# Attention and gated MLP on one core: output products of chunks 1 and 2 by seven block products, scores and P V in one TensorE visit

## The chip, the core and the metric

The kernel runs on one core of a Trainium2 chip. A core has five engines with their own instruction streams: PE (TensorE, matrix products into PSUM), DVE (VectorE), ACT (ScalarE), POOL (GpSimd, which works on SBUF alone) and SP, which issues most of the DMAs. They wait for each other through semaphores. The metric is the device time of one execution in microseconds; lower is better.

## What is computed

A sparse attention over 8 batches, 8 heads, 576 positions and head dimension 64, whose output, put together as 4608 tokens of width 512, goes through an RMS norm and a gated MLP with 1536 hidden units:

```python
scores = scale * np.matmul(q, k.transpose(0, 1, 3, 2))
mask_local = (rel >= 0) & (rel < stride)                          # heads 0 to 3, stride 32
mask_strided = (rel >= 0) & (pos[None, :] % stride == pos[:, None] % stride)   # heads 4 to 7
attn = softmax(np.where(masks, scores, -1e9))
x = np.matmul(attn, v)                     # then [4608, 512]
xn = x / rms * rms_g
g = xn @ w_gate                            # [512, 1536]
silu = g * (1.0 / (1.0 + np.exp(-g)))
out = silu * (xn @ w_val) @ w_out          # [1536, 512]
```

## The kernel before

**Chunks and units.** The 4608 tokens are 9 chunks of 512 columns (c = 0 to 8). The hidden width is 12 blocks of 128 (u). Every operand of a large product is split into a high half and a low half (fp32r), and a product is three matmuls: high by high, low by high, high by low. A plain gate or value product of one u is 4 blocks of 128 x 3 = 12 matmuls of 512 columns; a plain output product of one u is 4 x 3 = 12.

**Chunks 0, 1, 2** (`for c in range(NS1)`, near the end of `attn_moe`) are done plainly. For each u: `slot_g` and `slot_v` form g and v in one PSUM bank each (`g`, `v`), ACT takes tanh and DVE forms h = 0.5 (1 + tanh(g/2)) g v in the tile `e`; `slot_h` splits h into `hh` (ACT) and `hl` (POOL, line 1045), and `slot_o` (line 1055) adds 4 x 3 matmuls of that u into four accumulator banks a0 to a3, which are held for the whole chunk.

**Pairs of chunks** (3, 4), (5, 6) and (7, 8) are done as 2 x 2 block products by a Strassen-like scheme with seven products in place of eight. `plain_pair(c, beside)` does the first two pairs, `pair_of_chunks(7)` the last. A pair has a gate and value stage of twelve quads, `quad(q)` (line 1822), each of seven products of 6 matmuls with operands A11, A12, S1, S2, S3, S4, A22 (S1 is the sum of the second chunk's parts, S2 = S1 - A11), and then an output stage (line 2053) of seven products, A11, A12, S1, S2, S4, S3, A22 in that order, each of 2 x 6 x 3 = 36 matmuls. The output stage needs every h of the pair, sums of them (`hsum`, line 2028), splits of them (`split`, lines 1968 to 1972), and weights transformed once into DRAM: `transform_gv` and `transform_o` do that on DVE, POOL and ACT, spread over chunks 1 and 2. A quad uses the banks (g, a0, a2) or (v, a1, a3) by turns.

**Attention** runs beside all this, in units (b, p, j), 96 of them. From unit 20 on (`BT`) two units go together: a visit of TensorE for their scores (line 564, `step_e`), the masked row maximum on DVE (570), exponentials on ACT (577), normalising (607, 609), a 32 x 32 transpose on DVE (620), moves by DMA (623), and later a visit for P V of four units (line 798, `step_o`). Both kinds of visit use the two banks b0 and b1 of the tile `pair`. The profile shows two passes for each of these matmuls. `rms(c, ...)` then squares, adds, takes the square root (943), four reciprocals (946) and four scalings (950) for the 512 tokens of a chunk.

**Order.** Lines 418 to 441 give every attention unit a slot for its scores (`starts`) and for its P V (`outs`); `before(s)` and `behind(s)` list them beside slot s. This listing settles the dependencies. The real order of the instructions on each engine, and which engine does an operation that has a choice, is read from the packed table `ORDER` by `Plan.order` (line 283), which takes any listed operation next that the table names. In an output stage `between()` lists two slots after each product.

Of the kernel before, what the change touches and what calls it, by code (L numbers as in the profile page):

```python
# [47 lines left out]
TOW = ((1, 2), (1, 6), (1, 10), (2, 0), (2, 4), (2, 8))  # L48
# [8 lines left out]
GOFF = 0  # L57
FP = 99
# [119 lines left out]
    "c-rk*X>1(ld49fQ?%CPddzZ`QeIMc_k`gaT6iJDcMCzbKilV67mK0gC9XqmO$98JNZX7sH8n<!cI=1ZCIqJra8@nwW2TkibXi=nT(55NcB0vH(Kz<bMpB89;"  # L178
    "wBIqa(x0LY;2;UA1*M(iop0Xbd7k&3*~vE645LJlDkU??{+ffOUc*SG(hD7_(3ta0(@&ghI_cY;aD(x&qvaRf>otMpJ6CzY7aibf%8dj!ug*GVirc@=O=KB&"
    "nStP40!puea)Q9XT@-HmQ3^sH2J!j1w0q5*A|EnbfY=tjZ`BGJamhs>?NaPbo+eg-;JDR5XUwB0d4#&~7dcH6jEDuf9~wLMps<azZbo*x_^&M~vc;S5kNtb|"  # L180
    "u(yf<1KSSSoA^Kl?p~9j-3o#qaGR#-4_(>~ez!$Tw*b7?_&xq^mVZ0j^k;b2$fi?ltPqCZ%dt0-8TJ=%zSj6w`i=J*-bil>UaP~a@6fKVf5rbow&S%|e42j#"
    "D=&I2U-XcC{&TpFmlD^XxBbsN_uGO0x!;8U{Fl6mr(W}({dE3%>oZR#U&)O=3p4S;W9Dzw`_Ce2eCjg~KT|fIHlF;AkH9PZ8o&0~NAsWjT=MVvC!RZz#r;p0"
    "*~hM>pY}g7!0vsjf{(fPl|M)yO*}>)xa;ym52HY@k~0_XyO#Xu6Q{}3IA^6E-9UIbq_rPFaE9Y*@#Lik{qo%xH*jC_GR_~nH+vT6@5I`vb06?maGIu<FP}@E"
    "-nfd~`bLn&;VX$#chB*Y2RF`N+J5}X#({%4y=@6A8#_)-Wowr=N^5&DxjM0b|L()6KX_o@F?MX_!J|jnkv+%Q=={NhN9K<oe)T}pAzb{|tt*S!1LwA^J~y-H"
    "z+PmQ=J%}aC0Jj<mV@($jKdh2U9$IM=f1xEd)PwP-d(%z?V3A@$+?M6y0&u%R(A}Lvq$Q;wQe4tIDQ;snAtHuf24UDyLjU^Oixd2UO@fWuC0spTV^m$7U#zn"
    "D|5q`8J#&hI*lE72ZI}RI59GD@tD;&)=vh{p4s%>@^|{t^Z5<z@6G+B>zPeI&UGfcJDkn~nWx&?m)f><W-#B@-pMd}S5vvM1$UA=9CD$<uhf#Dxuyng3%p8x"
    "ZS81-vr#te2GkX6Q814qN0G2H$BwM-O%Y@doP?7|?AtdJy3;3pc)pFmSsim${9xI4uHb;_zzF`_G7{f5;hLNq<_^o*jv8i|oFPjmhG`mOWcS#iaBjpTm}X0K"
    "5L3HQH|JcckgXxV{dLPG?JVy#f6+KGf??ikrv{v`BRs^<Bpoa=cqe)1`a$ZfV2;?cGa!`D&CSi@+`_E0OHi#my$<6TifaqSag5E`d28p+oXIlVuv>6*d?%Ks"
    "17LL2r@Q{ZdJF5s#x%FK!#Ly|nq>X~-w@;;fjw+fi(;hDAYd3Xw_Y0Vhr79V$Uyhm9=q!_SjW0cC|V{N(8z(MkuGyD+e6x&e)RP*f*zwA!irC}v$i&Dp)DAu"
    "z#w7$sGzr(pym$#0hEfY6)kz%)MPY*r0YOJp%Z*_J)cbvR|e7N)lQIc1V!Pf2eSos*jNIsutcs@AZCW9x#LjAeREU6qv+xwU1r!ugxjJ-b)JD*Rs$ghCb<ND"  # L190
    "QLI64!#SI5hdV{U*FCJcM~|AIM+jR!!IwoySVE1DWri9Dc~ZdPw5ZjAUFpf(40dLx!w@2aVxcb284&{6ZnyNe*{NO&CQFNCxiu}#s1%W`E7?KT`=EW7@7hV%"
    "wQbwAUD%d&Dug*05QIn5t5^w-u)|p-ofIX<T+gBlM+nT?oXahqLe4adFlE?`!>REG2*5jgb5=XQ-9+U~a|(@NO*5;d`&v<~NuXS;E22<FzJzo-4STd=r)|5o"
    "QYzWS(y(0^dZ%Cy4wP&^x6td`U$cMUxqmZbryRRCF%?YOey>*_jH0!YXsI2r(C<!~y;gn2Hb=_l%5Zkr>N)~*e;<}|Mo)KZl6SN;r&(i;dg-YtVt5neKN4`@"
    "=55%Sf3}t!nAo#_aZj+cU>fu0E)T{Gx4}qYPf`nW+z}iQ`Np3lgn;9{B$}N>6B^2}e!sRXE{4go!ki)#A|X<g@DUoX_#O>}D7V59*>oG>RN$l5gu_Mly$nTI"
    "=MflQfDhX2F6txjGFJLO-Bij7-J}&bmgRK@zHKEOtJzLimws&F!jIfaCGn57*ZgwXM9GHm^D^U%G2`}s2?CcTIQ!90t)DRahyO$jla2|u{+5sMr5}**e~%7P"
    "?tFJ>H^G3_3(}20=HJ2y`{p3pjPIkB68u#Y@RzjyJEE{a1OL+!YAWWpkT1Mr6hX2enN&WVLKX;K7T`*}`0|U_uV07%7I~8x_&u=K)9B><ciP&%6@H1b=4QOz"
    "(DViJhZbHySixIwSa|a_hS&MmUWG_1%rC#vX}<ggy!1!!cnxoV1K)JtcDcB98^za6^7>bdufpc!%U=Y0nY<W?MGDCTf$RC63(pyYjT({u>jm(C_`HR`Bk5-;"
# [24 lines left out]
    "MM~977f#CnlO8KW7E!LMv<g<S&T4i<F9~Q|W^w~ugz5}vGp$EN+akJD8p;ClDqb}bv>qwNRBq^NW7$EBES15VBvR2hib1EBM6EB1Hp;nRn(A242c;}162xGZ"
    "MT$xg$%BTV!UoaWqcvAus5FHWtxCFFTBcM9<&NrgH0B1;9HTmV1sW1#S8b7~x~lEoP)k)Go!H1ubuq4NScFWf3B%%6sM;yht|(@6PNMDT7L;nqS5)L0psLX`"
    "wK|P~$fIr?32@Ya;^^b<q;8-yt(Jy{i)54vm+IF*abKZ2aK@rAx#}BAWT@;&QMXl{M593El`Fy44K0FLd>v&p>bq38B%Ry1nR2bnygFBCYH_UvERrRSsCd3o"
    "nbHzh{nJXJ?x|N&c+{G5(+m?gIE9_KAx2{X<$83w`4qV^#^_cQflt#f%DtXDxMrD7K92`0xv4vpb~$c2H@U7Cjuo4sssSXnmw$}tc`S0iO7A#APDxapD%ce&"
    "6|^EgC~2f|%hG-_ooW@n?f}YT)o0aUOr!X8KIJe>dDJ%bI2tvkC@9L~K}a_^C~Ms{5z~xoazrR5T2V<nO=+t0xMx!uYXymxjFPJiiSGM1A0yH58ut{{=BgBk"
    "=uI@+Sk-UM$r$kZTWfH2_Lkvm<xpAEtx%6rEGoAabRL%;Rkgk`ZYi8;NX16+w62@O&GOG9p^jh|PxMOgBe{$QfoM3<-*F(CJ#kyolNRExeM3pr{H*7yDtRJo"
    ">ReKOW8RBqKULCL=#`Fw>vj<hKe_>^QAUwftfj^>)%YTD)KQWck~$gsc}G({R(x$z{nMc0)kIgn;}J&#0(#Vn;!t)n3DL+}<uK>*(-w~xW15ycQkEM)R#&Lu"
    "LOT#Wtq~skr4d1irlfwN;?e1<P}As<g-4L74ra=+m{HMFWE7DC#Z9#4k+kS98a>ddhgwACWx9Lo(UhwpSN7X@Sd9RwClwx<=rE#3BQ3$P+sX_)9xQGMn4Waw"
    "r^*QTnqpe?Slo}ujo&bM{A!n1H+l3NPc;kae*-sUL~j"  # L230
)


class Plan:

    LAT = LATC
# [13 lines left out]
    def op(self, eng, cost, at, fn, reads=(), writes=(), bytes_=0, rel=0.0, lock=(), tab=None, port=False, chain=False, also=None, early=0.0):  # L253
        i = len(self.ops)
        self.early.append(early)
        self.lift.append(0.0 if chain else self.boost)
        deps = set()
        for r in reads:
            if r in self.writer:
                deps.add(self.writer[r])  # L260
# [2134 lines left out]
```

## Time and profile before

| | us |
|---|---|
| runs | 3062.59, 969.14, 969.25 |
| median | 969.25 |
| the profiled execution | 968.01 |
| its span, first to last instruction | 966.1 |
| PE busy | 949.1 |
| DVE busy | 760.4 |
| ACT busy | 612.3 |
| POOL busy | 291.5 |

By the places of its lines in the trace, the attention of batch 0 fills the first 43 us, chunk 0 lasts to about 147, chunks 1 and 2 to about 397, the quads of pair 3 to 545 and its outputs to 602, pair 5 to 735 and 790, the last pair to the end. A duration that the profile gives to a matmul covers its whole passage; the distance between starts is what it costs in a row of them.

### The profile page before, as it was taken

How to read it: one execution, taken by the hardware profiler on the slowest of the kernel's cores; microseconds unless marked ns; L12 is line 12 of the kernel's file. 1: busy time of each engine (PE TensorE's matmuls, PEld its weight loads, DVE VectorE, ACT ScalarE, POOL GpSimd, SP SyncE). 2: the span in 40 equal slices, each digit the busy share in tenths (PEclk: the TensorE clock that was granted, in tenths of full speed). 3: DMA queues.
4: the chain of work that ended last, by engine and by line, in shares of the span. 5: the costliest groups of instructions: out<-in, count | busy, mean ns of one | idle time of the engine just before them, and what ended most of it. 6: DMA issues, size and time to landing. Idle time of an engine off the chain costs nothing.

```text
span 966.1 us, 16212 instructions
## 1 busy us (share of the span) xinstructions
PE 949.1 (98%) x5138; PEld 763.6 (79%) x5138; DVE 760.4 (79%) x1786; ACT 612.3 (63%) x1706; POOL 291.5 (30%) x286
## 2 busy tenths in 40 slices
PE   8999999999999999999999999999999999999998
PEld 6777777878876888788888788888877778888886
DVE  4889899878778889668856999955589997457882
ACT  6899999875569655675737883644378734333330
POOL 7333332353344541422213322200023330012340
PEclk9899999999999999999999999999999999999999
DMA  9999677665458448245664779675546794692551
GB/s 297 362 354 378 226 259 241 223 206 182 152 178 254 145 144 271 67 142 179 230 216 139 242 249 351 230 246 193 167 155 197 256 358 171 247 327 88 174 172 68
DMA packets 99381, 210.99 MB, mean 218 GB/s; under 512 B 11040, under 2 KB 40416, under 8 KB 99296
## 3 DMA queue, kind: packets, MB, share of 16 engines
q1 hardware_dynamic: 98528, 209.10, 63.6%
q10 hardware_dynamic: 768, 0.85, 0.3%
q8 instruction: 41, 0.67, 0.3%
q14 instruction: 44, 0.36, 0.1%
HBM read 158.99 MB, written 47.19 MB: 213 GB/s over the span
## 4 chain that ended last, share of the span: by engine, by line
PE 84%; DMA 5%; ACT 5%; DVE 3%; issue 1%; SPq 0%; POOL 0%; ACTq 0%; DVEq 0%; POOLq 0%
PE acc L1822 10%; PE g L1003 9%; PE acc L1055 9%; PE v L1003 9%; PE g L1822 7%; PE v L1822 6%; PE acc L2053 4%; PE pair L564 3%; PE pair L1433 3%; PE v L1433 3%; PE g L1433 3%; PE pair L798 3%; PE v L2053 2%; PE g L2053 2%; PE acc L1433 2%; PE v L1598 2%
## 5 line engine op out<-in xcount | busy, mean ns | idle before, releaser
L1003 PE MATMUL g<-xh,wg 128*128 128x512 f32 x288 | 92.7, 403 | 4.6 <-ACT srt L943 2.5
L1055 PE MATMUL acc<-or,hh 128*128 128x512 f32 x288 | 91.1, 398 | 0.0
L1003 PE MATMUL v<-xh,wv 128*128 128x512 f32 x280 | 88.2, 396 | 0.0
L1045 POOL TENSOR_TENSOR hl<-e,hh 128x512 fp32r<-128x512 f32 x36 | 49.0, 1362 | 116.9 <-ACT hh L1036 99.0
L1003 PEld LDWEIGHTS g<-xh,wg 128*128 128x128 f32 x288 | 52.1, 189 | 18.7 <-DVE e L1018 3.2
L577 ACT ACTIVATE pp<-pp,my 96x128 f32<-96x128 f32 (+2 forms) x146 | 56.8, 395 | 11.4 <-DVE my L570 11.3
L1055 PEld LDWEIGHTS acc<-or,hh 128*128 128x128 f32 x288 | 53.0, 188 | 12.8 <-issue 0.6
L1003 PEld LDWEIGHTS v<-xh,wv 128*128 128x128 f32 x280 | 51.5, 188 | 12.4 <-DVE e L1029 0.5
L1003 PE MATMUL g<-xl,wg 128*128 128x512 f32 x144 | 56.2, 390 | 0.0
L1055 PE MATMUL acc<-or,hl 128*128 128x512 f32 x144 | 56.1, 390 | 0.0
L577 ACT ACTIVATE pT<-pT,my 96x128 f32<-96x128 f32 (+2 forms) x130 | 50.4, 391 | 6.8 <-DVE my L570 6.6
L1003 PE MATMUL v<-xl,wv 128*128 128x512 f32 x140 | 54.6, 390 | 0.0
L883 POOL TENSOR_TENSOR ssq<-ssq,srt 128x512 f32<-128x512 f32 x21 | 29.5, 1404 | 50.6 <-ACT srt L878 47.8
L564 PEld LDWEIGHTS pair<-xx,xx 64*96 64x96 f32 (+2 forms) x552 | 31.9, 167 | 14.3 <-issue 9.2
L564 PE MATMUL pair<-xx,xx 64*96 64x128 f32 (+2 forms) x552 | 39.8, 281 | 0.7 <-ACT raw L843 0.7
L1036 ACT CAST hh<-e 128x512 fp32r<-128x512 f32 x36 | 22.4, 621 | 26.0 <-DVE e L1029 18.0
L607 ACT ACTIVATE pp<-pp,my 96x128 f32<-96x128 f32 (+2 forms) x114 | 36.3, 394 | 3.4 <-DVE my L596 3.1
L570 DVE CUSTOM_DVE_ANT_0 pp<-pair,cb 96x128 f32<-96x128 f32 (+2 forms) x146 | 32.8, 282 | 5.9 <-PE pair L564 5.9
L570 DVE CUSTOM_DVE_ANT_0 pT<-pair,cb 96x128 f32<-96x128 f32 (+2 forms) x130 | 29.2, 281 | 8.4 <-PE pair L564 8.3
L1018 DVE SCALAR_TENSOR_TENSOR e<-e,g 128x512 f32<-128x512 f32 x36 | 24.5, 680 | 11.2 <-ACT e L1016 10.8
L1003 PEld LDWEIGHTS g<-xl,wg 128*128 128x128 f32 x144 | 27.1, 188 | 6.1
L1055 PEld LDWEIGHTS acc<-or,hl 128*128 128x128 f32 x144 | 27.0, 188 | 5.8
(819 smaller groups left out, 2864.7 us busy)
## 6 DMA issues: line engine op xcount, KB each, us to landing
wv<-wsv SPq DMA_DIRECT2D x29, 512.0 KB, 5.6
or<-wos SPq DMA_DIRECT2D x48, 256.0 KB, 3.6
or<-tg SPq DMA_DIRECT2D x22, 512.0 KB, 6.1
th<-tg SPq DMA_DIRECT2D x21, 512.0 KB, 6.0
tl<-tg SPq DMA_DIRECT2D x21, 512.0 KB, 5.8
wg<-wsg SPq DMA_DIRECT2D x19, 512.0 KB, 8.0
xx<-in_qT_dram SPq DMA_DIRECT2D x31, 288.0 KB, 4.7
xx<-in_kT_dram SPq DMA_DIRECT2D x28, 288.0 KB, 4.2
```

The costliest lines, as they stand in the source:

```text
L564: nc.tensor.matmul(out=sp[h][:, t].rearrange("q x k -> q (x k)"), lhsT=qt[r, q0:q0 + m], rhs=kt[r, k0:k0 + P], start=True, stop=True)
L570: nc.vector.tensor_tensor_reduce(out=PX[x][:m, :, g0 + 2 * h + t], in0=sp[h][:, t], in1=mk[t], scale=-0.125, scalar=3.0e38, op0=ALU.add, o ...
L577: nc.scalar.activation(out=v, in_=v, func=AF.Exp, scale=-1.0, bias=mx2[z][:m, u, h, t:t + 1], accum_out=su2_[z][:m, u, h, t, 0:1])
L607: nc.scalar.activation(out=w, in_=w, func=AF.Copy, scale=mx2[z][:m_, y, h, t:t + 1])
L798: nc.tensor.matmul(out=po[64 * h:64 * h + 64, x * 32 * nx:(x + 1) * 32 * nx].rearrange("d (x q) -> d x q", q=32), lhsT=vt_of(vt, p)[:n, h, ...
L883: op("Pool", pool(CH), at, lambda e: (nc.vector if e == "DVE" else nc.gpsimd).tensor_tensor(out=ssq, in0=ssq, in1=roots["srt"], op=ALU.add ...
L1003: nc.tensor.matmul(out=out, lhsT=wt[:, w, sl], rhs=xhl[x, kc], start=(kc == 0 and i == 0), stop=(kc == KC - 1 and i == 2))
L1045: (nc.vector if n == "DVE" or h else nc.gpsimd).tensor_tensor(out=hl[h], in0=e, in1=hh[h].bitcast(F32), op=ALU.subtract)
L1055: nc.tensor.matmul(out=acc[t], lhsT=x[h][:, sl], rhs=wt[:, w], start=(u == 0 and i == 0), stop=(u == NU - 1 and i == 2))
L1433: nc.tensor.matmul(out=banks[bk], lhsT=w, rhs=X[a, k].tile(y), start=start and k == 0 and i == 0, stop=stop and k == 1 and i == 2, skip_gr ...
L1822: nc.tensor.matmul(out=banks[bk], lhsT=w, rhs=xtile(a, k, y), start=start and k == 0 and i == 0, stop=stop and k == 1 and i == 2, skip_gro ...
L2053: nc.tensor.matmul(out=banks[bks[j]], lhsT=w.tile(v, k, j), rhs=x.tile(k, y), start=start and n == 0 and i == 0, stop=stop and n == KT - 1 ...
```

## The change

Chunks 1 and 2 keep their plain gate and value products, but all of their h is kept in SBUF (`slot_h1`) and their output products become the seven-product output stage of the pairs, which is moved out of `plain_pair` into a function `outputs` of its own. Chunk 2 takes its units in the order 11, 10, 9, 0 to 8. The slots behind it move by twelve. g and v of chunks 1 and 2 alternate between banks a2, a3 and g, v. P V of units from 24 on goes to a0 and a1 (one tile, `acc01`), a2 and a3 become two separate tiles, and the quads of pairs 3 and 5 use a2 and a3 alone beside g and v. A score visit and a P V visit that fall into one slot are one PE operation. The output weights are no longer read again for chunks 1 and 2; `transform_o` reads them from DRAM. The root of a chunk goes through bank a1 in place of g. The table `ORDER` is new throughout.

```diff
-TOW = ((1, 2), (1, 6), (1, 10), (2, 0), (2, 4), (2, 8))
+TOW = (14, 17, 20, 23, 26, 29)
+TGW = (13, 15, 16, 18, 19, 21, 22, 24)
+VSP = (12.0, 16.0, 26.0, 12.0, 12.0, 30.0, 12.0, 20.0)
+PVD = 2
+FU = 24
...
-        acc23 = ps.tile([P, 2, 512], F32, name="acc23")
...
+    acc = [acc01[:, 0], acc01[:, 1]] + [ps.tile([P, 512], F32, name=f"acc{t}") for t in (2, 3)]
...
+    slots = [9.0] * 12 + [5.9] * 24 + [4.9] * 12 + [9.9] * 12 + [4.9] * 12 + [9.9] * 12 + [4.9] * 12
+    t_of = [sum(slots[:x]) for x in range(len(slots) + 1)]
+    visits = {}
+    for k, (i0, i1, sa, sb_) in enumerate(((BS, 36, 12, 24), (36, 60, 24, 48), (60, 84, 48, 72), (84, last + 1, 72, 96))):
+        n = (i1 - i0) // 2
+        ta, tb_ = t_of[sa] + VSP[2 * k], t_of[sb_] - VSP[2 * k + 1]
+        for x in range(n):
+            t = ta + (tb_ - ta) * x / n
+            visits[max(y for y in range(len(slots)) if t_of[y] <= t)] = [i0 + 2 * x, i0 + 2 * x + 1]
...
-            d = where[i + PG - 1 - (i - PP0) % PG if i < last - 7 else i + (last - i) % 2] + PVL
+            late = next(x for n, x in ((36, 22), (60, 45), (84, 69), (last + 1, 90)) if i < n)
+            d = min([x for x in visits if x >= max(s + PVD, NU + 1)] + [max(late, s + PVD)])
             outs[d] = outs.get(d, []) + [i]
...
-                m8 = pair[:m, :, 508:508 + nt]
+                for hs, pr in joint(pn):
+                    m8 = pr[:m, :, 508:508 + nt]
...
+        if beside_:
+            op("PE", SC0 + length + sum(x[2] for x in beside_), 0, lambda: [x() for x in [y[0] for y in beside_] + [values]],
+               reads=reads + [y for x in beside_ for y in x[1]], writes=wk + [("S", 0), ("T", 0)], lock=("b0", "b1") + locks[:len(units)])
...
-    def bank_of(c, key):
+    def bank_of(c, key, x=0):
...
-        return bank[key[0]], key[0]
+        n = (key[0], {"g": "a2", "v": "a3"}[key[0]])[x]
+        return banks[n], n
...
+    def slot_h1(c, u, x):
+        out, bk = bank_of(c, ("v", u), x)
...
+        op("DVE", dve(CH), 0, lambda: nc.vector.scalar_tensor_tensor(
+            out=htile1(u, c - 1), in0=e(), scalar=0.5, in1=out, op0=ALU.mult, op1=ALU.mult), reads=[bk, ek],
+            writes=[hkey1(u, c - 1)] + [k for k in first if k != hkey1(u, c - 1)])
...
-            p, q_, r = (("g", "a0", "a2"), ("v", "a1", "a3"))[z]
+            p, q_, r = (("g", "a3", "a3"), ("v", "a2", "a2"))[z] if q < 2 else (("g", "a2", "a3"), ("v", "a3", "a2"))[z]
...
-        for m in "125637":
+        for m in "126537":
...
+    for c in (1, 2):
+        for x, u in enumerate(range(NU) if c == 1 else order2):
+            s = NU * c + x
+            slot_g(c, u, x % 2)
+            slot_v(c, u, x % 2)
...
+            beside(s)
+            slot_h1(c, u, x % 2)
+            roots_of(s, "a1", "A01")
+            if s in tslots:
+                transform_gv(tslots[s])
+            if s in TOW:
+                transform_o(TOW.index(s))
...
+    outputs(1, lazy1, htile1, hkey1, beside, (0, 1, 2, 3, 4, 5),
+            {"a": ("wg1", "wv1", "wg3", "wv3", "wg4", "wv4"), "b": ("wg0", "wv0", "wg2", "wv2", "wg5", "wv5"),
+             "c": ("X0", "wv7", "wg8", "wv8", "th0", "tl0")}, ("wg6", "wv6", "wg7", "X1", "X2", "X3", "or4"),
+            ["wg5", "wv5", "wg6", "wv6", "wg7"] + list(H2), ["wv7", "wg8", "wv8"])
```

`outputs` holds the seven products as `plain_pair` had them, and its lists name where operands (a, b, c) and weights lie and which gate and value weights are given back (`early` before the last product, `late` after it). X1 to X3 are the tiles of the x operands of the plain products.

## Rows read from the trace of the kernel before

**Rows 1.** Stretches: length, busy PE, PEld, DVE, ACT, POOL (instructions), clock, DMA share, GB/s

```profile
147.00:272.00 125.00, 123.42 (x712) 99.00 (x713) 103.21 (x283) 92.77 (x294) 49.78 (x47) 1.00 0.61 201
272.00:397.00 125.00, 121.77 (x726) 96.81 (x725) 106.21 (x296) 85.15 (x264) 53.64 (x51) 1.00 0.58 189
...
545.00:602.00 57.00, 56.82 (x285) 46.05 (x284) 55.18 (x109) 35.23 (x86) 13.48 (x12) 1.00 0.84 285
...
39.00:50.00 11.00, 11.00 (x55) 8.91 (x51) 8.71 (x29) 8.27 (x28) 3.65 (x3) 0.53 0.96 331
```

**Rows 2.** Chain of waits: start us, us, what; one block of six matmuls

```profile
421.55 1.36 PE v L1822 x6
```

**Rows 3.** Waits of PE: who, for whom, us in total, times, longest

```profile
PE g L1003 <- ACT srt L943: 2.5, 2, 1.9
PE g L1003 <- DVE e L1018: 2.1, 2, 1.5
...
PE acc L1433 <- DMA wg<-wsg: 0.4, 1, 0.4
```

**Rows 4.** Stretches of one line alone, L1055 first, then L2053: busy PE (matmuls)

```profile
0.00:966.10 966.10, 114.48 (x432) 79.95 (x432) 0.99 0.64 218
...
0.00:966.10 966.10, 118.50 (x504) 93.92 (x504) 0.99 0.64 218
```

**Rows 5.** Groups: line, engine, operation, tiles, shapes, count, busy us, mean ns, idle

```profile
L1972 DVE TENSOR_TENSOR or<-wv,or 128x512 fp32r<-128x512 f32 x8 | 5.3, 678 | 0.3 <-ACT or L1968 0.3
...
L1107 DVE TENSOR_TENSOR tt<-wg 128x512 f32<-128x512 f32 x6 | 7.7, 1281 | 0.0
...
L1045 POOL TENSOR_TENSOR hl<-e,hh 128x512 fp32r<-128x512 f32 x25 | 34.0, 1362 | 66.7 <-ACT hh L1036 66.7
```

**Rows 6.** Timeline of PE, a score visit: start us, us, line, tiles, count

```profile
450.03 0.39 PE L1822 MATMUL v<-xl,th 128*128 128x512 f32 x1
450.35 1.12 PE L564 MATMUL pair<-xx,xx 64*96 64x128 f32 x16
451.40 0.98 PE L1822 MATMUL acc<-wg,wg 128*128 128x512 f32 x3
452.21 0.63 PE L1822 MATMUL acc<-wv,wg 128*128 128x512 f32 x2
```

**Rows 7.** Timeline of PE, a P V visit

```profile
769.51 0.84 PE L2053 MATMUL g<-tl,wv 128*128 128x512 f32 x3
770.28 0.88 PE L798 MATMUL pair<-pp,vt 128*64 128x96 f32 x16
771.09 0.96 PE L2053 MATMUL v<-tl,wv 128*128 128x512 f32 x3
771.89 0.40 PE L2053 MATMUL acc<-wv,wg 128*128 128x512 f32 x1
```

**Rows 8.** Timeline of PE in the prologue, scores followed by P V

```profile
17.01 0.38 PE L672 MATMUL pair<-wg,xx 128*126 128x126 f32 x2
17.23 0.38 PE L672 MATMUL pair<-wv,xx 128*126 128x126 f32 x2
17.55 0.55 PE L804 MATMUL acc<-xl,vt 128*64 128x96 f32 x8
```

**Rows 9.** Instructions of line 689: count, ns min/median/max, first and last start, forms

```profile
L689 DVE TENSOR_SCALAR mx<-acc x9: 157/158/161, 10.2 to 35.5; 96x4 f32<-96x4 f32 x5, 108x4 f32<-108x4 f32 x2, 108x2 f32<-108x2 f32 x2
```

**Rows 10.** Timelines of PE, ACT and DVE: last P V of chunk 6, root, operand S1

```profile
561.24 1.53 PE L798 MATMUL pair<-pT,vt 108*64 108x128 f32 x24
...
578.08 0.69 ACT L943 ACTIVATE srt<-acc,few 128x512 f32<-128x512 f32 x1
...
604.67 0.69 DVE L1729 TENSOR_TENSOR wv<-or,wv 128x512 fp32r<-128x512 f32 x1
```

**Rows 11.** Groups of DVE from 147 to 397 us: reciprocals and scalings of the roots

```profile
L946 DVE RECIPROCAL srt<-srt 128x128 f32<-128x128 f32 x16 | 14.2, 917 | 0.0
...
L950 DVE SCALAR_TENSOR_TENSOR raw<-raw,few,srt 128x512 f32<-128x512 f32 x16 | 11.5, 736 | 0.1
```

More of the change, by code (lines that the diff above doesn't have):

```diff
@@ L182 @@
[L182 to L185, printed above, removed]
@@ L251, in __init__, with op @@
         self.boost = 0.0
-    def op(self, eng, cost, at, fn, reads=(), writes=(), bytes_=0, rel=0.0, lock=(), tab=None, port=False, chain=False, also=None, early=0.0):
+    def op(self, eng, cost, at, fn, reads=(), writes=(), bytes_=0, rel=0.0, lock=(), tab=None, port=False, chain=False, also=None, early=0.0, extra=()):
         i = len(self.ops)
@@ L772, in step_t, with step_o @@
         op(*(("DVE", dve(2 * nt * m)) if i in EVD else ("ACT", act(2 * nt * m, True))), at + 1500,
[L773 to L775 removed]
+           lambda e: [nc.scalar.copy(out=dv[:, hs], in_=pr[:n, :, 256:256 + nt * m]) if e == "ACT" else
+                      nc.vector.tensor_copy(out=dv[:, hs], in_=pr[:n, :, 256:256 + nt * m]) for hs, pr in joint(pn)], reads=[TK], writes=[tk], lock=locks, also=[])
+    def step_o(units, beside_=()):
         flight.difference_update(units)
@@ L870, in square @@
             lead = p == (0 if c < NB - 1 else 2)
-            assert not (lead and busy)
+            assert not (lead and busy), (c, p, busy)
             busy.add(c)
@@ L1165, in attn_moe, with lent @@
     loan = {}
-    def lent(n):
-        if n not in loan:
-            loan[n] = sb.tile([P, CH], F32, name=n)
-        return loan[n]
+    def lent(n, x=0):
+        if (n, x) not in loan:
+            loan[n, x] = sb.tile([P, CH], F32, name=n)
+        return loan[n, x]
     def temps_of(z):
@@ L2046, in plain_pair @@
-        ended = set()
-        def oproduct(x, w, bks, start, stop):
-            for j in range(2):
-                for n, k in enumerate(KO):
-                    def fn(j=j, k=k, n=n):
-                        for i, (v, y) in enumerate(((0, 0), (1, 0), (0, 1))):
-                            nc.tensor.matmul(out=banks[bks[j]], lhsT=w.tile(v, k, j), rhs=x.tile(k, y), start=start and n == 0 and i == 0,
-                                             stop=stop and n == KT - 1 and i == 2, skip_group_check=True)
-                    op("PE", 680, 0, fn, reads=w.key(k) + x.keys(k), writes=bank_keys(bks[j]), chain=True)
@@ L2256, in scores_of @@
                 x[3]()
+            for i in units:
+                step_d(i)
             return
@@ new lines, in attn_moe @@
+    for u in range(NU):
+        at, s = T(0, u), u
+        before(s)
+        slot_g(0, u)
+        if u == NU - 1:
+            slot_v(0, u)
+            convert(1, at + CVO)
+        behind(s)
+        if u < NU - 1:
+            slot_v(0, u)
+        if u > 0:
+            slot_o(0, u - 1, at + SOO)
+        slot_h(0, u)
+        roots_of(s)
+    for c in (1, 2):
[3 more added lines that the diff above has]
+            slot_v(c, u, x % 2)
+            if c == 1 and x == 0:
+                slot_o(0, NU - 1, 0)
+            if c == 1 and x == NU - 1:
+                convert(2, 0)
+            beside(s)
+            slot_h1(c, u, x % 2)
+            roots_of(s, "a1", "A01")
```

670 lines of the change are left out of this document (341 added, 329 removed).

## The prediction

> **What bounds the kernel now.** The profiled execution took 968.0 us, its span is 966.1 us; the median of the three runs is 969.25 us, 1.2 us more, so a sum made against the profile should come out about a microsecond low against a run. I read the page's busy times first: PE is busy 949.1 us of the span (98%), DVE 79%, ACT 63%, POOL 30%. Busy PE is not useful PE, so the next view is the table by stretch [rows 1]: in the two stretches that hold chunks 1 and 2, PE is busy 123.4 and 121.8 of 125 us at a granted clock of 1.00. Then the chain of waits: a block of six 512-column matmuls advances it by 1.36 us [rows 2], 0.2267 us each, one behind the other; that is the unit of price below. Last the waits of PE [rows 3]: none totals more than 2.5 us. So from about 50 us on the kernel is a queue of matmuls: taking matmuls out shortens it, and making other engines busier costs nothing until PE waits for them. DVE is where that would begin, with 103.2 and 106.2 of 125 us in these stretches and 55.2 of 57 us in the output stage of pair 3, which is the pattern of the new stage; yet PE was busy 56.8 of those 57 us [rows 1].
>
> **Part 1, output products of chunks 1 and 2.** Now each chunk takes 144 output matmuls: L1055 has 432 for chunks 0, 1 and 2. A pair done by seven block products takes 252: L2053 has 504 for two pairs [rows 4]. 2 x 144 - 252 = 36 matmuls fewer, 36 x 0.2267 = **8.2 us** off PE. No other matmul of the MoE changes its count.
>
> The new work is elementwise: 7 products x 6 operands are split into high and low halves (42 casts, 42 subtractions, where 24 of each go), 24 sums of h, 8 copies and 6 merges out of PSUM for 8 evictions. At 0.68 us [rows 5] the 42 + 24 + 6 are 49 us if DVE takes all. In return POOL loses 24 subtractions of 1.36 us [rows 5], 33 us. The cover is POOL: 24 operations moved there fill those 33 us again and leave DVE with 49 - 16 = 33 us more. DVE had 209 of 250 us in the two stretches; three score visits that lay in them (342 to 370 us) now fall behind them. I cost it at nothing for PE, because rows 1 show DVE at 97% with PE saturated; if that cover is gone, the late-root rival below is what it costs.
>
> **Part 2, scores and P V in one visit.** A score visit interrupts the 512-column stream: from 450.03 to 452.21 us there are four main matmuls (0.907 us) and 16 passes of 128 columns [rows 6], so the visit costs 2.18 - 0.91 = 1.27 us. At a quarter of 0.2267 a pass the columns are 0.91 of it; 0.36 is lost in going in and out. Around a P V visit, from 769.51 to 771.89, there are six main matmuls (1.36) and 16 passes of 96 columns (16 x 0.0425 = 0.68) [rows 7]: 2.38 - 1.36 - 0.68 = 0.34 lost. The placement code (lines 418 to 441) makes 38 such score visits from unit 20 on and 21 P V visits; the trace has as many. Worked through, the new placement gives 23 joined visits, 15 of scores alone and 5 of P V alone. Before: 38 x 0.36 + 21 x 0.34 = 20.8 us lost.
>
> No joined visit of this form is in the trace. Bounds: as cheap as a score visit (0.36, the seam free) gives 15.4 us, 5.4 us saved; as dear as both (0.70) gives 23.2, 2.4 us more than now. Nearest row: in the prologue eight score passes are followed at once by eight P V passes; a pair of passes starts 0.22 us after the last, but the first P V pair 0.32 us after [rows 8], so the seam takes 0.10, and with a little for the next pass I take 0.15. Joined 0.36 + 0.15 = 0.51: 23 x 0.51 + 15 x 0.36 + 5 x 0.34 = 18.8, **2.0 us** saved.
>
> The Trainium skill speaks against much of this (TensorEngine Tiling (Array Packing), Key Properties): changing the tiling mode drains TensorE. Scores use 64 rows of the array and P V 64 columns, so the seam is itself such a change. By that rule 59 visits are 118 changes of 20.8/118 = 0.18 us, the new plan has 23 x 3 + 20 x 2 = 109, and 1.6 us would be saved instead of 2.0. Our trace has a seam of 0.10 to 0.15 us, so it agrees that the seam is not free.
>
> **Part 3, what moves.** g and v of chunks 1 and 2 alternate between two banks each. PE's waits for the gate operation on g (2.1 us in 2 waits, the longer 1.5 near 396 us) [rows 3] come from the one bank: I take 1.5 us off, between 0 and 2.1. Units 2, 5, 8, 11 of the prologue reduce and copy two separate banks in place of one joint tile: four more small DVE operations at 0.16 us [rows 9] and as much again in fixed parts, 0 to 2; I take 0.6 us.
>
> The fourteen weight transforms now lie in chunks 1 and 2's products alone, on fewer temporaries, and those of w_out read from DRAM; they feed nothing before the output stage, so they are part of DVE's load above. SP's queue gets 42 loads of 256 KB for the stage, 14 loads of 512 KB that give the gate and value weights back, 8 stores, 6 loads of transformed weights and some 4 MB of q, k, v: 27 MB, where pair 3's stage moved 285 GB/s x 57 us = 16 MB at 84% of the DMA engines [rows 1]. Ten of the give-backs are for units that pair 3 uses 19 us or later and 12 weight loads can come early; the rest, 18 MB in the 65 us of stage and visits, is 277 GB/s. I take nothing.
>
> The boundary is the dear place. The last P V of chunk 4 is now listed after the fifth of the seven products, so two products (72 x 0.2267 = 16.3 us) and four products of pair 3 that need chunk 3 alone (5.4 us) lie between it and the first product that needs chunk 4: 21.8 us. At pair 5 this stands again. In the trace the same chain, from the last P V of chunk 6 at 561.24 us over the square root's end at 578.77 to the last half of operand S1 at 605.36, took 44.1 us [rows 10]. Dense it is 17.5 us to the root, four reciprocals of 0.92 and four scalings of 0.74 [rows 11], and three operations of 0.68: 26 us. So by the listing PE would wait 4 to 22 us, twice. But the listing is not the order: in before this P V was listed after the fourth product of pair 3 and ran at 561, some 19 us into products that began at 542, that is after little over two. Moved ahead as far (13 us) there are 35 us, and the dense chain fits. Such boundaries now cost tenths of a microsecond, as the 0.4 us for weights at the last one [rows 3], nearer to nothing; I take 1 us for each, **2.0 us**, between 0 and 44.
>
> **Sum.** 968.0 - 8.2 - 2.0 - 1.5 + 0.6 + 2.0 = **958.9 us**. By the page's rule it is 959.3.
>
> **Rivals.**
> *The root of chunk 4 (and 6) is late* (the other side). If DVE stays as full as in 545 to 602 us while X operands, splits and two roots all want it, the chain is nearer its 44 us than 26 and 35 us are too short: 9 us at each of two places, 18 in all, 958.9 - 2 + 18 = 975 us. The kernel is slower than before once the two waits exceed 11 us together, and by over 2% once they exceed 30. For it: DVE at 97%, and a two-input operation of the same size that took 1.28 us on average at one line [rows 5]; the long ones among those six run while POOL is busy. Against it: at pair 5's start, 601 us, the waits of PE name no operand of that pair. The skill has a rule here (Advanced Engine Details and Errata, VectorE Performance Modes): DVE's second SBUF port is shared with GpSimd and the two block each other; so handing DVE's work to POOL, my cover, lengthens what is left. That agrees with the 1.28 us.
> *Two banks too few.* The quads of pairs 3 and 5 now share a2 and a3 where they had a0 to a3. The bank of a gate product is asked for again four products (5.4 us) later; freeing it takes three operations of about 0.7. If DVE is behind by the 3.4 us between, PE waits; one DVE operation per quad, 24 x 0.68 = 16 us, gives 975 us. Nothing in the trace shows such a wait at the wider spacing.
> *DMA binds the new stage.* All 27 MB at the 331 GB/s of the busiest stretch [rows 1] take 82 us instead of 65: 976 us. Against it: most give-backs are not due.
> *The joined visits save nothing*: 2.0 + 2.4 us more, 963.3 us.
> *The new order also takes out old idle* (faster): the waits for the roots (2.5 us) and the half-speed stretch; from 39 to 50 us the clock was 0.53 [rows 1], 1.2 GHz, after PE had been idle and in short bursts, worth some 5 us. With no boundary wait: 958.9 - 2.0 - 2.5 - 5.2 = 949.2, and a free seam makes it 945.8.
>
> **Chances.** Forecast, 953 to 964 us (the joined visits saving nothing included): 0.55. Late root 0.17, banks 0.09, DMA 0.05, old idle 0.14. Low 949 leaves out some 0.08 of the last; high 970 leaves out about 0.12 of the first three, so 949 to 970 holds 8 in 10. A difference of 2% (19 us) is about what a measurement of this kernel can tell from no change: under 948.6 by the profile's time is only the end of the old-idle case, 0.08; over 987 only two dear boundaries, 0.04; the rest, 0.88, is within.
>
> **What would show it.** Right: 252 output matmuls for chunks 1 and 2 in place of 288; 43 visits; joined ones that lose about 0.5 us; PE without waits over 1 us at the ends of the output stages. Wrong: PE waiting for operands of pair 3 or 5 (ACT, DVE casts), for a2 or a3, or for weights from DRAM; another clock in the first 60 us, which no step above touches.

## The result

The changed kernel takes 956.3 us (median of 4 runs, 954.9 to 957.9) against 969.2 us of the kernel before, run beside it: a ratio of 0.987, interval 0.985 to 0.989. The forecast was 958.9 us, between 949 and 970, with 0.88 on less than 2% either way. The profiled execution took 954.9 us, its span is 953.1 us, where the profile before had 966.1.

Stretches of the changed kernel, columns as in [rows 1]: the products of chunks 1 and 2, their new output stage, and the 39 to 50 us that ran at half clock before.

```profile
154.00:327.00 173.00, 170.39 (x1025) 136.46 (x1025) 152.56 (x408) 117.82 (x379) 79.76 (x75) 1.00 0.59 199
327.00:397.00 70.00, 68.62 (x386) 54.48 (x386) 66.89 (x173) 58.17 (x182) 19.63 (x16) 1.00 0.84 280
...
39.00:50.00 11.00, 10.94 (x68) 8.86 (x68) 9.20 (x28) 10.79 (x33) 2.63 (x2) 1.00 0.89 331
```

In the new stage PE is busy 68.6 of 70 us beside a DVE at 66.9, as in the stage of pair 3 in [rows 1]. The clock in 39 to 50 us is 1.00, where it was 0.53.

The output products by line, as in [rows 4]: the plain form (chunk 0 alone now), then the seven-product form, three stages of 252.

```profile
0.00:953.10 953.10, 38.17 (x144) 26.35 (x144) 1.00 0.68 234
...
0.00:953.10 953.10, 177.87 (x756) 140.55 (x756) 1.00 0.68 234
```

144 + 756 = 900 in place of 432 + 504 = 936: 36 fewer. A block of six still advances the chain of waits by 1.36 us [rows 2]:

```profile
430.02 1.36 PE v L2093 x6
```

The waits of PE, as in [rows 3]:

```profile
PE v L1891 <- DVE wv L1080: 1.7, 1, 1.7
...
PE g L1034 <- DVE e L1050: 1.4, 2, 0.8
PE acc L1113 <- POOL or L2275: 1.2, 1, 1.2
PE g L1034 <- DVE wg L2275: 1.0, 1, 1.0
...
PE acc L1113 <- POOL hl L1104: 0.9, 1, 0.9
...
PE g L2093 <- ACT hh L1898: 0.7, 1, 0.7
```

The 2.5 us for the root are gone. In their place stands a row of waits for DVE and POOL: the first is at 325.6 us, at the door of the new output stage; the last, before pair 3, is for a bank that is still being copied out, not for a root. The three rows with L2275 (weight conversions) and L1104 (the low half of an h, for which chunk 0's output products in L1113 wait) belong to 130 to 165 us, the passage from chunk 0 to chunk 1.

Where the 13.0 us of span went can be counted from the starts of all matmuls in the two traces. I take the 51st 512-column matmul of the MoE as the border. From it on, both kernels run the same 576 score and 600 P V passes. A visit is counted with the first matmul behind it; a wait is a gap of over 0.25 us between two 512-column matmuls, or what a visit takes more than others of its size.

| us | before | after | difference | forecast |
|---|---|---|---|---|
| start of the 51st matmul | 61.82 | 56.69 | -5.1 | +0.6 |
| matmuls from there x 0.2267 | 800.25 (3530) | 792.09 (3494) | -8.2 | -8.2 |
| visits, without waits in them | 86.58 | 83.93 | -2.7 | -2.0 |
| waits | 8.90 | 12.16 | +3.3 | +0.5 (-1.5, +2.0) |
| the other gaps | 4.63 | 4.54 | -0.1 | 0 |
| last matmul to the end | 3.89 | 3.72 | -0.2 | 0 |
| span | 966.1 | 953.1 | -13.0 | -9.1 |

So the total came out near the forecast with two terms off in opposite directions: the first 60 us gained 5.1 where 0.6 were to be lost, and waits grew by 3.3 us where 0.5 was forecast. That the two partly cancel is luck.

### The profile page after: what moved, and what is told of

The parts are those of the page before. It is cut to its first block, busy times and chain, and to the rows that moved or that the text cites. A ratio compares the mean times of both kernels' runs of the same rounds, so it can differ in the third digit from the quotient of the medians.

```text
span 953.1 us, 16197 instructions
## 1 busy us (share of the span) xinstructions
PE 934.2 (98%) x5102; PEld 753.8 (79%) x5102; DVE 770.6 (81%) x1809; ACT 625.2 (66%) x1758; POOL 310.7 (33%) x294
## 4 chain that ended last, share of the span: by engine, by line
PE 84%; DVE 7%; ACT 5%; DMA 2%; issue 1%; ACTq 0%; SPq 0%; DVEq 0%
PE acc L2093 10%; PE acc L1891 8%; PE g L2093 7%; PE v L2093 7%; PE g L1034 6%; PE v L1891 5%; PE g L1891 5%; PE v L1034 5%; PE acc L1034 5%; PE v L1502 3%; PE acc L1502 3%; PE g L1502 3%; PE pair L582 3%; PE acc L820 3%; PE acc L1113 2%; PE g L1667 2%
## 5 line engine op out<-in xcount | busy, mean ns | idle before, releaser
L1034 PE MATMUL g<-xh,wg 128*128 128x512 f32 x192 | 61.2, 399 | 2.4 <-DVE e L1050 1.4
L1034 PE MATMUL v<-xh,wv 128*128 128x512 f32 x184 | 59.0, 401 | 0.9 <-DVE e L1088 0.6
L595 ACT ACTIVATE pT<-pT,my 96x128 f32<-96x128 f32 (+2 forms) x130 | 50.3, 391 | 0.5 <-DVE my L588 0.5
L1034 PEld LDWEIGHTS g<-xh,wg 128*128 128x128 f32 x192 | 35.0, 188 | 11.7 <-DVE e L1050 2.3
L873 ACT COPY raw<-acc 128x192 f32<-128x192 f32 (+16 forms) x97 | 22.3, 345 | 28.9 <-PE acc L820 26.8
L1034 PE MATMUL g<-xl,wg 128*128 128x512 f32 x96 | 37.5, 390 | 0.0
L1034 PE MATMUL acc<-xh,wv 128*128 128x512 f32 x104 | 32.7, 395 | 0.8 <-DVE or L1080 0.8
L1113 PE MATMUL acc<-or,hh 128*128 128x512 f32 x96 | 30.8, 400 | 1.2 <-POOL or L2275 1.2
L625 ACT ACTIVATE pT<-pT,my 96x128 f32<-96x128 f32 (+2 forms) x96 | 29.9, 392 | 3.0 <-DVE my L614 3.0
L1034 PE MATMUL acc<-xh,wg 128*128 128x512 f32 x96 | 30.1, 395 | 0.0
L2093 PE MATMUL acc<-wg,wv 128*128 128x512 f32 x102 | 28.7, 389 | 0.0
L2093 PE MATMUL acc<-wv,wv 128*128 128x512 f32 x102 | 28.6, 389 | 0.0
```

The source lines that it names most:

```text
L595: nc.scalar.activation(out=v, in_=v, func=AF.Exp, scale=-1.0, bias=mx2[z][:m, u, h, t:t + 1], accum_out=su2_[z][:m, u, h, t, 0:1])
L625: nc.scalar.activation(out=w, in_=w, func=AF.Copy, scale=mx2[z][:m_, y, h, t:t + 1])
L873: nc.scalar.copy(out=d, in_=s)
L1034: nc.tensor.matmul(out=out, lhsT=wt[:, w, sl], rhs=xhl[x, kc], start=(kc == 0 and i == 0), stop=(kc == KC - 1 and i == 2))
L1113: nc.tensor.matmul(out=acc[t], lhsT=x[h][:, sl], rhs=wt[:, w], start=(u == 0 and i == 0), stop=(u == NU - 1 and i == 2))
L2093: nc.tensor.matmul(out=banks[bk], lhsT=w, rhs=xtile(a, k, y), start=start and k == 0 and i == 0, stop=stop and k == 1 and i == 2, skip_gro ...
```

## Experiments

Of each edit the lines that matter are shown. Each change of order below acts on the decoded list of operations just before it is run. "Behind X" means that an operation is put behind operation X of that list, and an operation whose inputs are then late is put off until they are there. Times are compared on one chip; where the changed kernel itself did not run beside an experiment, its ratio to the kernel before, 0.987, stands for it and makes it 957 to 957.7 us.

**The changed kernel again**, as a yardstick for the next three.

> The changed kernel itself, beside the next three on one chip, so that they have a yardstick. Every theory expects the time already seen, 955 to 958 us, about 12.9 us under the kernel before, and a granted clock of 1.00 from 40 to 50 us in its profile.

Measured: 958.1 us against 969.7, ratio 0.987 (0.986 to 0.989). The result repeats in a second set of runs.

**Joined visits taken apart, P V later.**

```diff
-   lambda: [x() for x in [y[0] for y in beside_] + [values]]
+   lambda: [y[0]() for y in beside_]      # values: behind the next operation of TensorE
```

> The 23 joined visits are taken apart again: the P V passes run one product (three or more 512-column matmuls) after the scores, nothing else moves. Theory A (a join saves what the visits of the two traces say: 16 score passes with 16 P V passes cost 2.09 us joined against 1.29 + 1.03 apart, and likewise for the other sizes, 0.22 to 0.25 us each): 23 x 0.24 = 5.5 us longer, about 962 us. Theory B (the forecast's price: 0.36 + 0.34 lost apart, 0.51 joined): 23 x 0.19 = 4.4 us longer. Theory C (a join saves nothing, the seam costs as much as going out and in again): no difference.

Measured: 970.0 us, 11.9 us longer: more than any theory said. The count of matmul starts splits it. The visits take 90.9 us in place of 84.4; 2.2 us of that are waits inside them (0.5 before), so 23 joins are worth (6.5 - 1.7) / 23 = 0.21 us each. The other 7 us or so are waits (16.9 in place of 11.7 us between matmuls) and wider gaps; the next run takes the lateness of the P V away.

**Joined visits taken apart, scores earlier.**

```diff
+   early = {a: self.ahead[b] for a, b in zip(pe, pe[1:]) if b in self.ahead}
+   out.extend(early.get(i, []))           # the scores, ahead of the operation before
```

> The changed kernel with the 23 joined visits apart the other way round: the scores run one product earlier, the P V passes stay where they are, so that nothing comes later. Theory A (a join saves 0.22 to 0.28 us, and the other 5 us that were lost with the P V passes later are VectorE's and ScalarE's queues, which stand behind the late P V): 23 x 0.24 = 5.5 us longer than the changed kernel, 4 to 7 us, without new long waits. Theory B (apart costs 0.5 us a visit whatever comes first): 11 to 12 us longer, as with the P V passes later.

Measured: 965.1 us, about 8 us longer (ratio 0.995, 0.993 to 0.997), between the two theories. The visits take 89.2 us in place of 84.4, 0.4 us of it waits inside them (0.5 before): again 0.21 us a join. Waits between matmuls are 3.1 us more, in place of 5.1, so the late P V was part of the loss above, and not all of it. One place on TensorE, apart and, in the changed kernel, joined (start us, us, line, tiles, shapes, count):

```profile
403.78 0.84 PE L2098 MATMUL v<-wv,wg 128*128 128x512 f32 x3
404.55 1.12 PE L586 MATMUL pair<-xx,xx 64*96 64x128 f32 x16
405.60 0.98 PE L2098 MATMUL acc<-wg,wg 128*128 128x512 f32 x3
406.41 0.86 PE L2098 MATMUL acc<-wv,wg 128*128 128x512 f32 x3
407.20 0.88 PE L824 MATMUL acc<-pp,vt 128*64 128x96 f32 x16
408.01 0.97 PE L2098 MATMUL acc<-wg,wg 128*128 128x512 f32 x3
408.81 0.85 PE L2098 MATMUL acc<-wv,wg 128*128 128x512 f32 x3
```

```profile
400.49 0.84 PE L2093 MATMUL acc<-wv,wg 128*128 128x512 f32 x3
401.26 1.12 PE L582 MATMUL pair<-xx,xx 64*96 64x128 f32 x16
402.31 0.88 PE L820 MATMUL acc<-pp,vt 128*64 128x96 f32 x16
403.12 0.97 PE L2093 MATMUL acc<-wg,wg 128*128 128x512 f32 x3
403.93 0.85 PE L2093 MATMUL acc<-wv,wg 128*128 128x512 f32 x3
```

Apart: 403.78 to 406.41 less six matmuls is 1.27 us, 406.41 to 408.81 less six is 1.04, together 2.31. Joined: 400.49 to 403.93 less six is 2.08. The join saves 0.23 us here.

**36 matmuls more.** The repeated product reads some operands that have been replaced meanwhile, so one output block of chunks 1 and 2 is not the product's; the time is what counts.

```diff
+   if again and j == 0 and n == KT - 1:   # first product of the stage, first bank
+       for k2 in (KO[m] for _ in range(2) for m in range(KT)): ...three matmuls
```

> The changed kernel with 36 matmuls more: in the output stage of chunks 1 and 2 the first bank's 18 matmuls of the first product run three times on the same operands (the last time counts), so the stage has 288 as before. Theory A (TensorE is a queue of matmuls in this stage too): 36 x 0.2267 = 8.2 us longer than the changed kernel. Theory B (VectorE bounds the new stage, which is 96% busy in it, and TensorE has slack there): clearly less than 8.2 us, down to 4, because the other engines catch up meanwhile and the waits of the stage (1.9 us at 325.6, 0.8 at 395.9) shrink.

Measured: 968.0 us, 10.3 us longer (ratio 0.998, 0.997 to 0.999). Theory A's 8.2 are there and nothing is caught up; the rest is waits, the longest of them new:

```profile
PE g L1896 <- DMA wg<-to: 1.6, 1, 1.6
```

L1896 is the line of the added matmuls: they wait for the load that replaces an operand which they read again. So this wait comes from the way in which the matmuls were repeated, and says nothing of the DMA of the stage as it is.

**One bank for the gate products.**

```diff
-   n = (key[0], {"g": "a2", "v": "a3"}[key[0]])[x]
+   n = (key[0], {"g": "g", "v": "a3"}[key[0]])[x]
```

> The changed kernel with one PSUM bank for the gate products of chunks 1 and 2 in place of two (the value products keep two). Theory A (the forecast's price of the single bank, 1.5 us, from the waits of the kernel before): 1 to 2 us longer than the changed kernel. Theory B (two banks are worth much more where VectorE is near full: each of 24 gate products would wait for its tanh and its gate operation): 5 us or more longer. Theory C (nothing: the value product between two gate products hides it): within 0.5 us.

Measured: 1001.2 us, 43 us longer (ratio 1.032, 1.029 to 1.035). Theory B, by far:

```profile
PE g L1049 <- DVE e L1065: 10.8, 8, 2.4
PE g L1049 <- DVE hl L1065: 9.7, 8, 2.2
PE v L1906 <- DVE wv L1095: 2.9, 1, 2.9
```

The order was searched for two banks, so this is the price of the bank in this order, not in the best order for one. It holds some lost clock too: behind such waits the granted clock is 0.5 in four stretches between 224 and 351 us, 17 us in all, which is worth at most half of that.

**The last P V of chunk 4 later.**

```diff
+   seq = self.settle(self.behind(seq, [1885], pe[pe.index(1885) + 8]))
```

> The changed kernel with the last P V passes of chunk 4 (371.4 us) put 8 half products, 5.4 us, later in TensorE's order. Theory A (the chain from there over the root to the first operand of pair 3 that needs chunk 4 fits with about a microsecond to spare; in the trace that product starts at 404.6 us and its last operand is ready near 404): TensorE waits some 4 us more at the start of pair 3, 4 to 5 us longer in all. Theory B (the boundary has slack, its 0.8 us is another wait): within 1 us. Theory C (VectorE's order behind it jams as well): 8 us or more.

Measured: 961.3 us, 3.5 us longer (ratio 0.990, 0.988 to 0.992), the size of theory A, but not at its place. The wait at the start of pair 3 is 0.84 us as before, and the product that first needs chunk 4 does not wait. The P V, the root's sum and that product, here and then in the changed kernel:

```profile
380.26 1.53 PE L842 MATMUL acc<-pT,vt 108*64 108x128 f32 x24
...
390.04 0.39 PE L964 MATMUL acc<-srt,onesr 128*128 128x512 f32 x1
...
410.48 0.39 PE L2115 MATMUL g<-wg,th 128*128 128x512 f32 x1
```

```profile
371.38 1.53 PE L820 MATMUL acc<-pT,vt 108*64 108x128 f32 x24
...
385.16 0.40 PE L942 MATMUL acc<-srt,onesr 128*128 128x512 f32 x1
...
404.62 0.39 PE L2093 MATMUL g<-wg,th 128*128 128x512 f32 x1
```

The P V runs 8.9 us later (5.4 by the order, the rest are waits in front of it), the sum 4.9, the product 5.9: the chain from the P V to the product took 33.2 us and fits into 30.2. What is lost lies in the stage ahead: without the P V in between TensorE comes to its later products sooner, and waits 1.3, 1.1 and 0.9 us for their operands (two from DVE, one weight load).

**An h moved ahead on VectorE.**

```diff
+   seq = self.settle(self.behind(seq, [1665, 1687], 1552))   # subtraction and maxima behind the h
```

> The changed kernel with one place of VectorE's order altered: at 324.4 us the h of chunk 2's eleventh unit runs before a subtraction of 1.8 us and four row maxima instead of after them. Theory A (the 1.9 us wait of TensorE at 325.6, the longest of the changed kernel, is this h in VectorE's queue and nothing else): 1.5 to 1.9 us shorter than the changed kernel. Theory B (the operands behind it are late too, so that the wait moves on): no difference within 0.5 us.

Measured: 957.7 us, ratio 0.987: no difference in the median. In the profile the wait falls from 1.7 to 0.7 us, but it moves on, as theory B has it: the score passes that follow now wait for the row maxima that the edit put back.

```profile
PE v L1912 <- DVE wv L1101: 0.7, 1, 0.7
...
PE pair L603 <- DVE my L609: 0.6, 1, 0.6
```

The h no longer stands behind the subtraction, but two operations ahead of it had grown in this execution, and the queue was late again:

```profile
320.90 2.55 DVE L1826 CAST xh<-wv 128x512 fp32r<-128x512 f32 x1
323.55 1.59 DVE L1828 TENSOR_TENSOR xl<-wv,xh 128x512 fp32r<-128x512 f32 x1
```

The next run shows what makes them long.

**Everything of the stage on VectorE.**

```diff
+   seq = [(i, "DVE" if i in self.mine and e == "Pool" and "DVE" in self.ops[i][0] else e) for i, e in seq]
```

> The changed kernel, with all sums and differences of the output stage of chunks 1 and 2 that run on GpSimd (some 17, between 303 and 388 us) given to VectorE at their place in the order. Theory A (GpSimd is the cover that the forecast named, and VectorE is 96% busy): VectorE gets 17 x 0.68 = 11.6 us more in a stretch where it is idle for some 7 us, and the kernel becomes 4 us or more longer. Theory B (the two engines block each other: nine operations of VectorE take 5.5 us more than their 0.68 us each in the stage, all beside GpSimd's): what moves over is given back by shorter operations, and the time stays within 1.5 us.

Measured: 956.2 us, ratio 0.986 (0.984 to 0.989): the same time. Theory B. The stretch in the changed kernel and here:

```profile
303.00:389.00 86.00, 84.26 (x503) 66.91 (x501) 79.98 (x207) 74.71 (x231) 33.02 (x28) 1.00 0.78 255
```

```profile
303.00:389.00 86.00, 85.53 (x505) 67.51 (x504) 83.10 (x220) 74.15 (x229) 12.71 (x13) 1.00 0.78 256
```

POOL is relieved of 20 us; DVE runs 13 operations more (at 0.68 us each 8.8 us) and is busy only 3.1 us longer. And the wait of 325.6 us is gone, while waits of 0.6 us and less came up at 315.7 and 390 to 392 us. Why it is gone, the same operations show, in the changed kernel (DVE, then POOL) and here:

```profile
321.43 1.65 DVE L1866 TENSOR_TENSOR wv<-wg,or 128x512 f32<-128x512 f32 x1
...
324.44 1.77 DVE L1807 TENSOR_TENSOR wv<-or,wv 128x512 fp32r<-128x512 f32 x1
...
326.98 0.67 DVE L1080 SCALAR_TENSOR_TENSOR wv<-e,v 128x512 f32<-128x512 f32 x1
...
321.18 1.35 POOL L1866 TENSOR_TENSOR wg<-wg,wv 128x512 f32<-128x512 f32 x1
322.49 1.74 POOL L1866 TENSOR_TENSOR or<-or,wv 128x512 f32<-128x512 f32 x1
324.31 1.36 POOL L1866 TENSOR_TENSOR wv<-wv,wg 128x512 f32<-128x512 f32 x1
```

```profile
321.58 0.69 DVE L1867 TENSOR_TENSOR wv<-wg,or 128x512 f32<-128x512 f32 x1
...
323.12 0.68 DVE L1808 TENSOR_TENSOR wv<-or,wv 128x512 fp32r<-128x512 f32 x1
...
324.87 0.69 DVE L1081 SCALAR_TENSOR_TENSOR wv<-e,v 128x512 f32<-128x512 f32 x1 [0.23 <-PE v L1035]
```

Beside POOL the two DVE operations took 1.65 and 1.77 us, alone 0.69 and 0.68, and the h that TensorE waits for comes 2.1 us earlier. In the changed kernel's stretch all eight 128x512 TENSOR_TENSOR operations of DVE that took over 0.8 us overlap an operation of POOL.

**Three places mended.**

```diff
+   seq = self.behind(seq, [1665, 1687], 1552)
+   seq = self.behind(seq, [857], 868)
+   seq = self.settle(self.behind(seq, [2032], 2033))
```

> The changed kernel with three places of its order mended: the h of 324 us ahead of VectorE's subtraction and maxima as in the earlier run, the last h of chunk 0 ahead of a subtraction at 162.5 us, and at the start of pair 3 the product into bank v ahead of the one into bank g, whose copy is still running. If each wait of TensorE there is only what its row says: 1.0 + 0.6 + 0.7 = 2.3 us shorter than the changed kernel, which should show in the waits of its profile and hardly in the median. If the waits move on to the next operand: no difference.

Measured: 958.0 us, ratio 0.988 (0.986 to 0.989): not shorter. The third place worked (0.84 to 0.28 us before pair 3). At the first the wait fell from 1.7 to 1.2 us only, and the score passes behind it waited 0.6 us, as in the earlier run. The second was a miss of mine: the subtraction moved is the one at 161.9 us, the low half of chunk 1's x, which TensorE wants itself, and the wait there grew from 0.8 to 2.1 us:

```profile
PE g L1057 <- DVE xl L1032: 2.0, 1, 2.0
```

**The pauses of the kernel before filled.**

```diff
+   plan.fills = {455: (512, 128), 185: (256,)}   # dummies behind these two operations
```

> The kernel before, with three dummy matmuls on TensorE in its two pauses at 36.2 and 38.2 us (512, 128 and 256 columns of four passes, about 0.85, 0.21 and 0.43 us of work that nothing reads). Theory A (some 5 us of the gain come from the clock: in the kernel before it is granted at half from 39 to 50 us because TensorE had paused before): the granted clock from 40 to 50 us becomes 1.00, and the kernel before gets about 5 us faster, 964 us. Theory B (the clock has nothing to do with the pauses, or the work there waits for other engines anyway): the time stays within 1 us of 969, whatever the clock does.

Measured: 965.9 us, 3.8 us shorter (ratio 0.997, 0.995 to 0.998), but single executions lie between 964.0 and 970.5. Their mean granted clock parts them: the three at 0.994 took 969.4 to 970.5 us, the seven at 0.998 to 1.000 took 964.0 to 967.3 us, with a median of 965.5. All 19 executions of the kernel before beside them are at 0.992 to 0.995. So where the slow clock stayed out, theory A's gain is there, 4.2 us. The profiled execution, 969.6 us, is one of the three and still has the slow clock, only later:

```profile
39.00:45.00 6.00, 5.71 (x39) 4.71 (x39) 4.81 (x15) 6.00 (x24) 2.20 (x3) 0.72 1.02 390
...
42.00:52.00 10.00, 10.00 (x43) 7.88 (x42) 7.33 (x22) 7.22 (x16) 3.57 (x3) 0.51 1.00 364
```

**A pause put into the changed kernel.**

```diff
+   seq = self.behind(seq, [454, 455], 201)
```

> The changed kernel, with the two products of chunk 0 that it runs at 34.9 to 36.2 us put behind the P V passes of 39 us, so that TensorE pauses about 2.7 us in all between 32.5 and 39 us instead of 1.3, as in the kernel before (2.0). Theory A (the pauses bring the half clock): the granted clock falls to 0.5 for some 10 us after it, and the kernel gets about 5 us longer, 961 us. Theory B (the order of work is what gained the 5 us, not the clock): the clock stays 1.00 and the time grows by no more than the 1.4 us of the two products.

Measured: 960.9 us, 2.8 us longer (ratio 0.990, 0.989 to 0.992). The clock falls:

```profile
32.00:37.00 5.00, 2.45 (x25) 1.42 (x21) 4.75 (x13) 4.98 (x14) 1.00 (x2) 1.00 1.02 412
...
39.00:45.00 6.00, 6.00 (x19) 4.59 (x19) 2.14 (x3) 5.50 (x19) 0.00 (x0) 0.51 0.91 357
```

PE was busy 2.45 of the 5 us before (3.7 in the changed kernel), then 0.51 for the next six. The 51st matmul starts 4.0 us later than in the yardstick. Theory A in kind, somewhat smaller.

**The kernel before as a stream.** A dummy here writes over the P V result of one prologue unit, so part of the attention output is not the reference's.

```diff
+   plan.fills = {455: (512, 128), 185: (256,), 192: (512,)}
+   seq = self.settle(self.behind(seq, [196], 204))
```

> The kernel before with its pauses of 36 to 39 us filled as in the run before this one (dummies of 512, 128 and 256 columns), a further dummy of 512 columns (0.85 us) behind the P V passes of 39 us, and the first value product in front of the score passes of 41 us, so that no half microsecond without wide matmuls is left between 33 and 43 us. Theory A (the clock falls where TensorE pauses or runs only narrow passes, and its fall is what the kernel before loses there): the granted clock from 40 to 50 us is 1.00 in the profile, and the time is 4 us under the kernel before in all executions, not in some of them. Theory B (something else sets the clock): it falls again at about 42 us, and the executions scatter between 964 and 970 us as with the three dummies alone.

Measured: 971.8 us, 2.1 us longer than the kernel before (ratio 1.002, 1.001 to 1.003): both theories miss. TensorE now waits 1.1 us for a square root on ACT, at full clock; the clock falls behind that wait, between 45 and 46 us, and a wait of 1.2 us for row maxima on DVE follows:

```profile
39.00:45.00 6.00, 4.37 (x32) 3.05 (x32) 2.77 (x11) 4.79 (x21) 1.80 (x2) 1.00 0.94 355
...
46.00:54.00 8.00, 6.85 (x40) 5.24 (x36) 6.66 (x20) 4.32 (x8) 1.26 (x1) 0.61 0.69 206
```

## Why the prediction was right, and where it was not

*Part 1, 36 matmuls at 0.2267 us: right.* The table has -8.16 us by their count, and the other gaps, where a wrong price would show, differ by 0.1. Putting 36 back cost 10.3 us, 8.2 of it the matmuls themselves. That the elementwise work costs TensorE little is right too, but the reason was wrong. I named POOL as the cover and charged DVE with what POOL did not take. Giving all of it to DVE changes nothing in the time: the 8.8 us of work that POOL takes over shorten DVE's busy time by only 3.1, since operations that DVE keeps get longer beside POOL. The rule that I had put under a rival (the Trainium skill, Advanced Engine Details and Errata, VectorE Performance Modes: GpSimd and two-port VectorE instructions block each other) fits, with 0.69 against 1.65 us for one operation; this is an operation with two inputs, which the note itself does not name. The rule should have stood in the cost of Part 1: there the cover is not another engine but DVE's own reserve of a few microseconds.

*Part 2, the joins: right in number and price, low in total.* The trace has 24 joined visits, 14 of scores and 4 of P V alone: the 23, 15 and 5 worked out, with one P V visit that happens to run right behind a score visit. The joined visit above loses 2.08 - 0.91 - 0.68 = 0.49 us, where 0.51 was forecast; taking the joins apart costs 0.21 us each, where 0.19 was forecast. So the seam of about 0.15 us, taken from eight passes of the prologue [rows 8], carries over to passes of other shapes. Some of that is luck: the score passes of that row use 128 rows of the array (128*126), so it does not show the change from 64 rows to 64 columns that a joined visit makes. The seam is not free, as the rule on the drain says (the Trainium skill, TensorEngine Tiling (Array Packing), Key Properties). Most of the table's 2.7 us is in these visits: beyond its columns a score visit loses 0.36 us in the traces, a P V visit 0.31 (0.34 in the forecast) and a joined one 0.47. Over all of them that is 20.2 us before and 17.7 after, 2.5 us less. What the forecast did not have: the join also binds the order. Apart, with the same passes, the rest of the order lost some 3 to 7 us more in waits.

*Part 3, the second bank: the term was mis-sized because it was asked the wrong question.* I took off 1.5 us for the waits that one bank causes in the kernel before. Such waits still total 1.4 us after. But output products no longer stand between two gate products, and with one bank the new loop, in its present order, loses 43 us. The bank doesn't remove an old wait; it prevents the one that the change would bring.

*The boundaries: right in size at pair 3 (0.84 us for 1.0), for another reason; none at pair 5.* The wait is for the last copy out of bank g, and one swap of two products took two thirds of it away. The chain over the root, which I took as the dear place, has slack: 33.2 us from the P V, and 30.2 still do. The rivals of a late root and of a bound DMA have no wait in the profile that would bear them out; in the new stage the DMA moved 280 GB/s, where 277 was worked out. For two banks too few there are two small ones in pair 3, 0.6 us for bank v and 0.4 for bank g, where the rival had 16 us. A wait of a microsecond for a weight load of the new stage, other than the one that the 36 added matmuls make for themselves, appears with the late P V alone (1.3 us).

*What was missing in the sum: waits outside the places I looked at.* 3.3 us more instead of 0.5. The longest, 1.7 us at the start of the output stage, is VectorE's queue beside POOL. Most of the others, some 7 us in all, lie between 130 and 165 us, where DVE is busy 34.7 of 35 us, with weight conversions and the root of chunk 1 among its work. I had counted the conversions as load only. No run takes that load away, so its part in these waits is argued, not shown.

*The first 60 us: a rival that came true and was not in the sum.* "The new order also takes out old idle" was given 0.14, and its 5 us of half clock are about what the table has (-5.1). The root waits of 2.5 us went as well. The total stayed near the forecast because the extra waits took about 3 us back. Had the 5.2 us been taken into the sum, it would have been 953.7 us by the profile's time, where 954.9 was measured; the evidence [rows 1] was there, but nothing in the diff named the prologue's order except that the table ORDER is new throughout. The clock can be most of the 5.1 us: in the kernel before with its pauses filled, whose order is the old one, the seven executions without the long slow stretch are 4.2 us shorter. A pause that brings the slow clock back costs 4.0 us at the 51st matmul and 2.8 us at the end. How much the better order adds stays open; streaming further in the kernel before only exposed waits for ACT and DVE.

## What to carry to other kernels

When work between two uses of a buffer is taken out, price the buffer in the new loop, not by its waits in the old one. Before another engine is counted as cover, compare the lengths of the same operations beside it and without it. An order that is searched anew can change any stretch with visible idle, so such a stretch belongs in the sum with a share, not only among the rivals.

## What the hardware showed

GpSimd as a helper gave little in this stage: 13 operations taken back by VectorE cost it 3.1 us instead of 8.8. The granted clock of TensorE fell to half (1.2 GHz) behind pauses that were short: 1.1 us at most in the kernel before, and in the filled one, with no pause over 0.3 us, behind some five microseconds without a 512-column product of the MoE, in which it ran narrow passes and the dummies. In these it stayed down for about ten microseconds, and for about seven behind the pause put into the changed kernel. In the profile of the changed kernel run again it fell behind the wait at the door of the output stage, to 0.50 from 327.8 to 331.2 us.
